# Attention over a cached K and V: scores with the keys on the partitions, exp without the row maximum, row sums from a column of ones in V

## Chip, cores and metric

The kernel runs on one core of a Trainium2 chip. The metric is device microseconds of a whole execution, lower is better. Medians are over all runs of a job, and all ratios below are the mean time of one kernel's fast runs over the mean of the other's fast runs of the same rounds.

Engines: PE is TensorE (PEld its weight loads), DVE VectorE, ACT ScalarE, POOL GpSimd, SP the sync engine that issues DMAs.

## The reference, cut

```python
# two independent problems A and B; B=16, Sq=80, D=576, Hq=32, Hkv=16, Sk=512, Dh=128, bf16
q = (x @ wq).reshape(B, Sq, Hq, Dh)                        # 2 query heads share one K/V head
scores = einsum("bhqd,bhkd->bhqk", q, k) * Dh ** -0.5
p = softmax(scores, axis=-1)
o = einsum("bhqk,bhkd->bhqd", p, v)
out = o.reshape(B, Sq, Hq * Dh) @ wo                       # A and B concatenated on the last axis
```

## The kernel before

The work is cut into 128 "units": one batch and four K/V heads (eight query heads) each. A unit has 4 x 160 rows of queries. The rows are tiled as four tiles of 128 rows, plus one tile that collects the four remainders of 32 rows by column tiling of PE. All operations are listed with a time key; sorting by it gives each engine's program, and semaphore waits are derived from reads and writes.

```python
def em_qk(e, ...):                      # scores: queries on partitions, 512 keys along the free axis
    if k == 0:                          # the four 32-row remainders, in one 128-row tile
        for g4 in range(4):
            last = e.matmul(ps[32*g4:32*g4+32, sbk, :], lhsT=qT[:, qsl, bl, g4*160+128:g4*160+160],
                            rhs=kT[:, ks, :, g4*128:(g4+1)*128], tile_position=(0, 32*g4), ...)
    else:
        last = e.matmul(ps[:, sbk, :], lhsT=qT[...128 rows...], rhs=kT[...], start=True, stop=True)
def em_max(e, ...):  return e.tensor_reduce(negmax[...], ps[:, sbk, :], op=max, negate=True)     # DVE
def em_exp(e, ...):  return e.activation(p_sb[:, psl, :], ps[:, sbk, :], AF.Exp,
                                         bias=negmax[...], accum_out=rowsum[...])                 # ACT
def em_rcp(e, ...):  return e.reciprocal(rinv[...], rowsum[...])                                  # DVE
def em_nrm(e, ...):  return e.tensor_scalar(p_sb[...], p_sb[...], rinv[...], 1.0, mult, mult)     # POOL
def em_tr(e, ...):   # four PE transposes of 128x128: p has to have the keys on partitions
def em_ptev(e, ...): return e.tensor_copy(pT[...], psb[...])                                      # DVE
def em_pv(e, ...):   # four accumulating matmuls, lhsT=V chunk, rhs=pT (160 columns)
# ... [cut] q projection (QB split 480+160 columns), output projection in two passes of 16 heads
S.add("sp", t_k - ..., em_ldk, ...)     # K by DMA transpose, five slots (buffers; NK = 5)
S.add("sp", t_v - ..., em_ldv, ...)     # V, four slots (NV = 4), the same queue
```

## Time and profile before

| | before |
|---|---|
| median of 3 runs | 816.34 us (814.7 to 817.53) |
| span of the profiled run | 812.5 us, granted clock 1.000 |
| PE / DVE / ACT / POOL busy | 98 / 84 / 79 / 53% |
| moved by DMA | 168.5 MB by the kernel's queue |

First, lines of the page of the kernel before: busy times, then rows of 40 equal slices (busy tenths; GB/s), the chain of waits that ended last, and groups (line, engine, operation, tiles, shapes, count, then busy us and mean ns of one, then idle time before it).

```profile
PE 797.9 (98%) x8940; PEld 620.6 (76%) x8940; DVE 680.2 (84%) x1617; ACT 643.4 (79%) x1725; POOL 433.0 (53%) x647
...
PE   7999999999999999999999999999999999999998
...
GB/s 228 243 245 283 249 235 268 260 254 219 190 214 182 224 231 214 207 162 223 180 199 240 245 219 230 237 259 223 224 200 191 200 195 214 199 187 172 156 29 37
...
PE 90%; DVE 5%; DMA 3%; SPq 0%; issue 0%; POOL 0%; ACT 0%; POOLq 0%
...
L452 POOL TENSOR_SCALAR p_sb<-p_sb,rinv 128x512 bf16<-128x512 bf16 x640 | 430.5, 695 | 354.6 <-DVE rinv L449 354.6
L445 ACT ACTIVATE p_sb<-ps,negmax 128x512 bf16<-128x512 f32 x640 | 442.3, 691 | 83.4 <-DVE negmax L441 65.3
L441 DVE TENSOR_REDUCE negmax<-ps 128x1 f32<-128x512 f32 x640 | 434.4, 679 | 4.5 <-PE ps L436 2.9
...
L458 PE MATMUL ps<-ident,p_sb 128*128 128x128 bf16 x2560 | 248.5, 220 | 4.6 <-DVE negmax L441 3.5
```

Everything else stands in PE's shadow: PE's row is all nines but for its two ends, and the chain is 90% PE. The 220 ns of one 128-column transpose is a latency, not a cost, because matmuls overlap: their starts in the trace are 56 ns apart. So PE has to be counted by start-to-start times. Next, the windows view of the same kernel: stretch and its length, busy us of each engine with the number of instructions, granted clock, DMA share, GB/s.

```profile
core 0: us, PE busy (x) PEld busy (x) DVE busy (x) ACT busy (x) POOL busy (x), PEclk, DMA share, GB/s
...
30.00:110.00 80.00, 78.52 (x862) 56.09 (x859) 78.61 (x191) 73.62 (x206) 53.60 (x80) 1.00 1.08 253
110.00:200.00 90.00, 88.75 (x1012) 69.80 (x1009) 74.58 (x176) 74.07 (x200) 47.29 (x71) 1.00 1.08 251
200.00:400.00 200.00, 200.00 (x2262) 156.59 (x2260) 172.05 (x411) 163.88 (x437) 109.50 (x163) 1.00 0.91 204
400.00:530.00 130.00, 130.00 (x1476) 102.06 (x1475) 113.91 (x274) 105.77 (x282) 72.15 (x108) 1.00 1.01 227
```

(The DMA share adds up the times of all packets, so it can pass 1.)

### The profile page before, as it was taken

To read this page: it belongs to the slowest core of one execution; us is meant where nothing else is said; L and a number is where in the kernel's file an instruction comes from. 1 tells how busy PE (TensorE), PEld (TensorE's weight loads), DVE (VectorE), ACT (ScalarE), POOL (GpSimd) and SP (SyncE) were. 2 spreads that over 40 slices of the span, in tenths; PEclk is the share of its full clock that TensorE was granted. 3 is DMA by queue.
4 is the path that set the end of the run, shared out by engine and by line. 5 is a ranking of instruction groups with operands and counts; after the bars stand their busy time and mean duration, and the time that the engine had idled before them with its cause. 6 is when DMAs were issued, how large, how long until landed. Compare 5 with 4: busy or idle time off the path is not lost.

```text
span 812.5 us, 23206 instructions
## 1 busy us (share of the span) xinstructions
PE 797.9 (98%) x8940; PEld 620.6 (76%) x8940; DVE 680.2 (84%) x1617; ACT 643.4 (79%) x1725; POOL 433.0 (53%) x647
## 2 busy tenths in 40 slices
PE   7999999999999999999999999999999999999998
PEld 4677678777777777877777777777777778777778
DVE  3899988888888889888888889888888888988872
ACT  2899888888878778888887887888887788888860
POOL 1466665455555546555555555555465455555650
DMA  9999999999897999979789999999978879977601
GB/s 228 243 245 283 249 235 268 260 254 219 190 214 182 224 231 214 207 162 223 180 199 240 245 219 230 237 259 223 224 200 191 200 195 214 199 187 172 156 29 37
DMA packets 363629, 169.94 MB, mean 209 GB/s; under 512 B 278017, under 2 KB 354305, under 8 KB 363521
## 3 DMA queue, kind: packets, MB, share of 16 engines
q1 hardware_dynamic: 363520, 168.46, 90.9%
q8 instruction: 73, 1.20, 0.6%
q14 instruction: 36, 0.29, 0.1%
HBM read 98.37 MB, written 2.95 MB: 125 GB/s over the span
## 4 chain that ended last, share of the span: by engine, by line
PE 90%; DVE 5%; DMA 3%; SPq 0%; issue 0%; POOL 0%; ACT 0%; POOLq 0%
PE ps L335 20%; PE ps L546 19%; PE ps L458 18%; PE ps L501 16%; PE ps L436 12%; PE ps L431 5%; DVE negmax L441 3%; DVE pT L466 1%; DMA kT<-in_A_k_cache_dram 1%; DMA v_sb<-in_A_v_cache_dram 1%; DMA wq_sb<-in_A_wq_dram 1%; PE ps L259 1%; POOL p_sb L452 0%; SPq L292 0%; DVE rinv L449 0%
## 5 line engine op out<-in xcount | busy, mean ns | idle before, releaser
L452 POOL TENSOR_SCALAR p_sb<-p_sb,rinv 128x512 bf16<-128x512 bf16 x640 | 430.5, 695 | 354.6 <-DVE rinv L449 354.6
L445 ACT ACTIVATE p_sb<-ps,negmax 128x512 bf16<-128x512 f32 x640 | 442.3, 691 | 83.4 <-DVE negmax L441 65.3
L441 DVE TENSOR_REDUCE negmax<-ps 128x1 f32<-128x512 f32 x640 | 434.4, 679 | 4.5 <-PE ps L436 2.9
L466 DVE COPY pT<-ps 128x512 bf16<-128x512 bf16 x512 | 209.3, 409 | 93.3 <-PE ps L458 92.6
L458 PE MATMUL ps<-ident,p_sb 128*128 128x128 bf16 x2560 | 248.5, 220 | 4.6 <-DVE negmax L441 3.5
L501 PE MATMUL ps<-pT,v_sb 128*128 128x160 bf16 x2048 | 225.3, 233 | 2.6 <-DMA v_sb<-in_A_v_cache_dram 1.3
L458 PEld LDWEIGHTS ps<-ident,p_sb 128*128 128x128 bf16 x2560 | 175.4, 98 | 57.2 <-DVE qT L347 21.6
L501 PEld LDWEIGHTS ps<-pT,v_sb 128*128 128x128 bf16 x2048 | 169.0, 98 | 63.9 <-DVE qT L347 3.6
L335 PE MATMUL ps<-xT,wq_sb 128*128 128x480 bf16 (+1 forms) x1280 | 214.4, 300 | 1.6 <-DMA wq_sb<-in_A_wq_dram 0.9
L436 PE MATMUL ps<-kT,qT 128*128 128x512 bf16 x512 | 194.0, 379 | 0.0
L546 PE MATMUL ps<-wo_sb,oT 128*128 128x192 bf16 x1920 | 175.7, 246 | 0.0
L546 PEld LDWEIGHTS ps<-wo_sb,oT 128*128 128x128 bf16 x1920 | 158.6, 98 | 0.0
L335 PEld LDWEIGHTS ps<-xT,wq_sb 128*128 128x128 bf16 x1280 | 107.0, 98 | 45.0 <-DVE qT L347 0.9
L513 ACT CAST oT<-ps 128x320 bf16<-128x320 f32 x256 | 108.9, 425 | 35.2 <-PE ps L501 32.9
L445 ACT ACTIVATION_READ_ACCUMULATOR p_sb<-ps,negmax 128x1 f32 x640 | 128.1, 200 | 0.0
L342 ACT ACTIVATE qT<-ps 128x480 bf16<-128x480 f32 (+1 forms) x128 | 71.8, 561 | 25.6 <-PE ps L335 25.5
L464 DVE COPY pT<-ps 128x512 bf16<-128x512 bf16 x128 | 52.9, 413 | 1.3 <-PE ps L458 1.3
L431 PE MATMUL ps<-kT,qT 128*32 128x512 bf16 x512 | 51.2, 390 | 1.4 <-DMA kT<-in_A_k_cache_dram 1.4
L436 PEld LDWEIGHTS ps<-kT,qT 128*128 128x128 bf16 x512 | 50.1, 98 | 0.7
L347 DVE TENSOR_SCALAR qT<-ps 128x160 bf16<-128x160 f32 (+1 forms) x128 | 41.5, 324 | 3.8 <-PE ps L335 3.7
L566 DVE TENSOR_TENSOR osb<-ps,acc 128x192 bf16<-128x192 f32 x60 | 21.0, 349 | 15.3 <-PE ps L546 12.2
L431 PEld LDWEIGHTS ps<-kT,qT 128*32 128x32 bf16 x512 | 13.1, 92 | 14.9 <-DMA kT<-in_A_k_cache_dram 1.6
(16 smaller groups left out, 77.5 us busy)
## 6 DMA issues: line engine op xcount, KB each, us to landing
v_sb<-in_A_v_cache_dram SPq DMA_DIRECT2D x64, 512.0 KB, 4.5
v_sb<-in_B_v_cache_dram SPq DMA_DIRECT2D x64, 512.0 KB, 4.5
wq_sb<-in_A_wq_dram SPq DMA_DIRECT2D x16, 512.0 KB, 5.5
wq_sb<-in_B_wq_dram SPq DMA_DIRECT2D x16, 512.0 KB, 5.5
wo_sb<-in_A_wo_dram SPq DMA_DIRECT2D x8, 576.0 KB, 5.4
wo_sb<-in_B_wo_dram SPq DMA_DIRECT2D x8, 576.0 KB, 4.8
out_dram<-osb SPq DMA_DIRECT2D x60, 48.0 KB, 2.1
xs<-in_A_x_dram SPq DMA_DIRECT2D x2, 720.0 KB, 5.1
```

The source lines that it names most:

```text
L335: last = e.matmul(ps[:, bank, 0:n1 - n0], lhsT=wq_sb[:, wsl, ck, i * 128:(i + 1) * 128], rhs=xT[:, xsl, ck, n0:n1], start=(ck == 0), stop= ...
L342: return e.activation(qT[:, qsl, b0:b0 + nb, col:col + 80], ps[:, bank, 0:n1 - n0].rearrange("p (b s) -> p b s", b=nb), AF.Identity, scale ...
L431: last = e.matmul(ps[32 * g4:32 * g4 + 32, sbk, :], lhsT=qT[:, qsl, bl, g4 * 160 + 128:g4 * 160 + 160], rhs=kT[:, ks, :, g4 * 128:(g4 + 1) ...
L436: last = e.matmul(ps[:, sbk, :], lhsT=qT[:, qsl, bl, gl * 160:gl * 160 + 128], rhs=kT[:, ks, :, gl * 128:(gl + 1) * 128], start=True, stop ...
L441: return e.tensor_reduce(negmax[:, si:si + 1], ps[:, sbk, :], axis=AX.X, op=AluOpType.max, negate=True)
L445: return e.activation(p_sb[:, psl, :], ps[:, sbk, :], AF.Exp, bias=negmax[:, si:si + 1], scale=1.0, accum_out=rowsum[:, ss, col:col + 1])
L452: return e.tensor_scalar(p_sb[:, psl, :], p_sb[:, psl, :], rinv[:, ss, col:col + 1], 1.0, op0=AluOpType.mult, op1=AluOpType.mult)
L458: last = e.transpose(psb[:, tb, j * 128:(j + 1) * 128], p_sb[:, psl, j * 128:(j + 1) * 128], ident[:])
L466: return e.tensor_copy(pT[:, pts, gl, :, 0:128], psb[:, tb, 0:512].rearrange("p (j n) -> p j n", j=4))
L501: last = e.matmul(ps[:, ob, off:off + 160], lhsT=v_sb[:, vs, gl, j * 128:(j + 1) * 128], rhs=pT[:, pts, gl, j, :], start=(j == 0), stop=(j ...
L513: return e.copy(oT[:, hb:hb + 4, bl * SQ:(bl + 1) * SQ], ps[:, ob, 0:320].rearrange("p (h s) -> p h s", h=4))
L546: last = e.matmul(ps[:, bank, 0:DC], lhsT=oT[:, h, r * 128:(r + 1) * 128], rhs=wo_sb[:, h, c3 * DC:(c3 + 1) * DC], start=(hi == 0), stop=( ...
```

## The change

The intent is to drop the transposes of p. If the scores come out with the keys on the partitions, exp of them is already the operand that P x V needs. Then the row maximum (now along partitions) is not to be had cheaply; it is left out, and a check at the end sends the program to the old code, kept as a general path, if any row sum is out of range. The row sum comes from V widened by a column of ones, and the output is normalised and transposed (5 tiles per unit, instead of 20 tiles of p). Because V needs its 129th column, POOL copies each V into a padded tile. K has four slots instead of five, V three; V is loaded from ACT's queue, and the q projection is split 320+320 columns.

```diff
-NK = 5
-NV = 4
+NK = 4
+NV = 3
+OP_ = 130
...
+        def em_s(e, ts=ts, sbk=sbk):                     # three key chunks of 128, 160 query columns each
+            for c, t in enumerate(ts):
+                last = e.matmul(ps[:, sbk, c * 160:(c + 1) * 160], lhsT=kT[:, U % NK, j, g * 128:(g + 1) * 128],
+                                rhs=qT[:, goct % 2, bl, g * 160:(g + 1) * 160], start=True, stop=True)
+        def em_exp(...): return e.activation(P[:, psl, 0:k, :], ps[...480 columns...], AF.Exp, scale=SCALE)
...
+        add("act", t_v, em_ldv, ...)                     # V from the ACT queue
+        add("pool", t_p, em_vp, ...)                     # v_sb[:, vps, :, 0:128] <- v_in; column 128 is one
+            def em_pv(...):  # x4 per g: lhsT=P[128 rows], rhs=v_sb[..., 0:129]
+        def em_pr(...):      # remainders: 16 matmuls, lhsT=P[..., 128:160], tile_position=(0, 32 * g)
+            def em_rcp(...): return e.reciprocal(rinv[...], ps[:, bank, 128::OP_])
+            def em_nrm(...): return e.tensor_tensor(o_sb[...], src, sc, AluOpType.mult)
+        def em_tr(...):      # five transposes of o_sb
...
+        with e.If_eq(regs[name], 0):                     # the flag says that a row sum was out of range
+            g_run(e, name)                               # the old code
```

## The prediction

> **What bounds the kernel now.** TensorE. The page puts PE at 98% of an 812.5 us span; the windows view shows PE busy 100.0 of 100 us from 200 to 700 us, at granted clock 1.00, while VectorE is at 84%, ScalarE 79%, GpSimd 53%. The chain of waits gives 90% to PE lines, 5% to DVE and 3% to DMA. Busy matmul records overlap, so I cost PE by start-to-start times in the trace: 512 columns 216 ns, 480 203, 192 82, 160 69, 128 56. The Trainium skill, "TensorE: Matmul & The Clock Gate", Back-to-back issue gap, gives N/2.4 + 2.5 ns; the trace agrees to 1 ns. Summed: q projection 174 us, scores of full tiles 111, the 32-row remainder tiles 54, transposes of p 143, PV 142, output projection 158, x transposes 6: 788 us. Remaining 24 us: start (first real matmul at 5.6 us, steady work near 16 us) and small gaps.
>
> The remainder tiles cost more than their columns. Going from a full matmul into the four 32-column ones takes 149 ns instead of 56, and the last of them 322 instead of 216: about 200 ns per visit. The skill's "TensorEngine Tiling (Array Packing)", Key Properties, says changing the tiling mode drains the engine; this trace agrees.
>
> **What the change does.** Removed: 2560 p transposes (143 us of PE), their 640 evictions (262 us DVE), 640 row maxima (434 us DVE), 640 accumulator reads (128 us ACT), 640 GpSimd normalisations (431 us), 256 oT casts on ACT (109 us).
> PE afterwards, by the same rule:
> - scores 2048 x 160 columns: 2048 x 69 = 142 (was 165 with remainders)
> - PV 2048 x 129 columns at 56: 115
> - PV remainders, 16 tiled matmuls of 129 columns per unit: 200 ns of mode change plus four groups estimated at 85 each, 540 ns x 128 = 69 (least certain)
> - transposes of o, 640 x 56: 36
> - q projection 174, output projection 158, x transposes 6, unchanged
> Sum about 700 us, against 788.
>
> Off the path: exp becomes 683 activations of 480 columns without bias pointer or accumulator; an activation of that size takes 569 ns, so about 390 us, plus 128 V-load issues (about 0.43 us each now) on ACT: below 500 us. VectorE: evictions of q, normalisation and oT, about 3 us per unit of 5.5. GpSimd repacks V, 2048 elements; from 695 ns per 512 at most 2.8 us per unit. The V-load issue on ACT waits for that copy, but 12 tiles of lookahead cover about 4 us. DMA moves the same 168 MB, now at about 230 GB/s; before, 40 us stretches reach 273, so it is near but not limiting.
>
> **Time.** 700 us plus the 24 us of start and gaps, plus some 4 us of slower start (V loads compete with the first wq) and 3 us for flag load and branch over the general path: **731 us**, 714 to 762 eight times in ten. Faster by over 2%: 0.96; within 2%: 0.03; slower: 0.01. General path not taken.
>
> **What would show it.** PE still near 98%, DVE near 55%, ACT near 65%; matmul spacing 69 (scores), 56 (PV), no p transposes; remainder block near 0.54 us; every mid-kernel window near 100% PE. Chain almost all PE.
>
> **What would make it wrong.** Tiled weight loads that do not overlap in the PV remainders (up to 0.9 us per unit, +45 us); GpSimd's copy over 4 us, stalling ACT and then PE; K transposes arriving late with four slots rather than five at a 13% higher rate, shown as PE waiting on kT DMA; a failed check, running everything twice.

## The result

| | before | changed | ratio of fast runs |
|---|---|---|---|
| median | 816.22 us (4 runs, the three above among them) | 752.43 us (749.74 to 767.18, 4 runs) | 0.9213, 95% [0.9177, 0.9248] |

It is faster by 8%, inside the predicted range, but 21 us above the predicted 731. The execution profiled first was in the slow state (span 765.4 us, clock 0.972), so the unchanged file was run again for a profile in the fast state. That is the first experiment, and its profile is the one shown here.

Expected of the repetition: 

> The changed kernel once more, for a profile in the fast state. Both theories need it: if the K transposes (or the DMA behind them) are what PE waits for, about 750 us with PE waits on kT of 15 to 30 us and a slower start (scores near 22 us instead of 15); if the 15 us between the slow and the fast runs are only clock, the stalls stay as long as in the slow profile (about 40 us after the start) and only the half-clock time shrinks.

Measured: median 753.98 us (744.57 to 755.01), ratio 0.9251, 95% [0.9221, 0.9282]. Its profiled run, fast, has a span of 742.8 us and is the quickest of its five by 8.5 us; keep that in mind wherever this profile is compared. Lines of its page:

```profile
PE 708.2 (95%) x10093; PEld 619.1 (83%) x10093; DVE 365.2 (49%) x974; ACT 390.9 (53%) x752; POOL 245.3 (33%) x136
...
PE   5987989979999999999999999999999999999996
...
PEclk8998999999999999999999999999999999999999
...
GB/s 253 262 263 266 283 266 249 248 226 243 229 212 234 236 241 245 255 228 191 252 219 253 230 284 267 240 262 273 261 212 241 242 197 269 217 202 186 171 13 35
...
PE 83%; DMA 15%; DVE 1%; SPq 0%; issue 0%; ACT 0%
...
L858 ACT ACTIVATE P<-ps 128x480 bf16<-128x480 f32 (+1 forms) x683 | 374.1, 570 | 304.1 <-PE ps L853 288.7
L887 POOL COPY v_sb<-v_in 128x2048 bf16<-128x2048 bf16 x128 | 242.7, 1896 | 460.5 <-PE ps L919 429.3
L853 PE MATMUL ps<-qT,kT 128*128 128x160 bf16 x2048 | 253.7, 233 | 19.2 <-DMA kT<-in_A_k_cache_dram 16.5
L908 PE MATMUL ps<-v_sb,P 128*128 128x129 bf16 x2048 | 205.4, 222 | 0.0
L919 PE MATMUL ps<-v_sb,P 128*32 128x129 bf16 x2048 | 54.3, 226 | 0.0
```

DMA's share of the chain went from 3 to 15%, and PE's row has dents, all but the last in its first quarter. The windows of the same run, beside those of before, say where:

```profile
core 0: us, PE busy (x) PEld busy (x) DVE busy (x) ACT busy (x) POOL busy (x), PEclk, DMA share, GB/s
...
30.00:110.00 80.00, 68.71 (x978) 57.27 (x976) 41.21 (x108) 45.11 (x85) 29.95 (x16) 0.94 1.16 267
110.00:200.00 90.00, 84.81 (x1211) 74.54 (x1209) 42.25 (x111) 47.49 (x95) 28.44 (x15) 0.98 1.17 242
200.00:400.00 200.00, 200.00 (x2921) 176.44 (x2918) 105.39 (x282) 112.44 (x214) 70.16 (x37) 1.00 1.03 230
400.00:530.00 130.00, 126.93 (x1846) 111.49 (x1835) 66.60 (x180) 70.10 (x134) 43.87 (x24) 1.00 1.18 260
```

Between 30 and 110 us PE stands still for 11 us while DMA moves 267 GB/s, the most of these four stretches. The longest such wait, in the timeline (start, length, engine, line, what; in brackets the idle time before it and what ended it):

```profile
45.68 9.87 SPq L880 DMA_TRANSPOSE kT<-in_A_k_cache_dram  x1
...
53.38 0.41 PE L908 MATMUL ps<-v_sb,P 128*128 128x129 bf16 x4
...
60.27 0.56 PE L853 MATMUL ps<-qT,kT 128*128 128x160 bf16 x3 [6.48 <-DMA kT<-in_A_k_cache_dram]
...
60.62 1.54 PE L798 MATMUL ps<-xT,wq_sb 128*128 128x320 bf16 x5
```

The issue of one K transpose holds the sync queue for 9.87 us (its median in this run is 3.9), PE finds no K, and after 6.48 us of waiting the next five q projection matmuls of 320 columns take 1.54 us where they take 0.84 elsewhere in this run. That is the clock. The clock records of the trace have 6.8 us at 0.5 from 58.2 us on, and further ones after the waits at 98 and 158 us: 24.5 us at half clock in all, of which about 11 belong to the cold start and the end. The Trainium skill, "TensorE: Matmul & The Clock Gate", Part 1, says that an idle window drops PE to half clock; this trace agrees. So a wait on DMA is paid twice, once while PE stands and once while it is cold. In the slow profile the waits and other gaps over 0.45 us add up to 47.7 us against 31.5 in the fast one, and the half clock to 44.8 against 24.5 us. Of the two readings in the expectation the first held: in the fast profile PE waits 19.2 us for K and the first scores come at 21.3 us, and the stalls shrank together with the half clock.

### The profile page after: what moved, and what is told of

It reads as the page before. It is cut to its first block, busy times and chain, and to the rows that moved or that the text cites. A ratio compares the mean times of both kernels' runs of the same rounds, so it can differ in the third digit from the quotient of the medians.

```text
span 765.4 us, 22766 instructions
## 1 busy us (share of the span) xinstructions
PE 714.9 (93%) x10093; PEld 623.6 (81%) x10093; DVE 365.2 (48%) x974; ACT 390.7 (51%) x752; POOL 244.9 (32%) x136
## 3 DMA queue, kind: packets, MB, share of 16 engines
q10 hardware_dynamic: 67584, 67.12, 31.5%
HBM read 98.37 MB, written 2.95 MB: 132 GB/s over the span
## 4 chain that ended last, share of the span: by engine, by line
PE 81%; DMA 17%; SPq 0%; DVE 0%; ACT 0%; issue 0%
PE ps L798 20%; PE ps L980 19%; PE ps L853 17%; PE ps L908 15%; DMA kT<-in_A_k_cache_dram 11%; PE ps L919 5%; DMA kT<-in_B_k_cache_dram 4%; PE ps L945 3%; DMA xs<-in_A_x_dram 1%; DMA out_dram<-osb 1%; PE ps L946 1%; PE ps L736 1%; ACT P L858 0%; SPq L767 0%; DVE qT L805 0%
## 5 line engine op out<-in xcount | busy, mean ns | idle before, releaser
L858 ACT ACTIVATE P<-ps 128x480 bf16<-128x480 f32 (+1 forms) x683 | 373.8, 570 | 325.5 <-PE ps L853 310.2
L887 POOL COPY v_sb<-v_in 128x2048 bf16<-128x2048 bf16 x128 | 242.3, 1893 | 483.3 <-PE ps L919 443.4
L853 PE MATMUL ps<-qT,kT 128*128 128x160 bf16 x2048 | 255.5, 235 | 31.6 <-DMA kT<-in_A_k_cache_dram 24.9
L798 PE MATMUL ps<-xT,wq_sb 128*128 128x320 bf16 x1280 | 220.9, 305 | 3.4 <-DVE qT L805 2.9
L908 PE MATMUL ps<-v_sb,P 128*128 128x129 bf16 x2048 | 206.8, 223 | 0.0
L853 PEld LDWEIGHTS ps<-qT,kT 128*128 128x128 bf16 x2048 | 161.3, 98 | 50.9 <-issue 33.7
L805 DVE CAST qT<-ps 128x320 bf16<-128x320 f32 x248 | 121.4, 489 | 91.3 <-PE ps L798 91.2
L908 PEld LDWEIGHTS ps<-v_sb,P 128*128 128x128 bf16 x2048 | 144.3, 99 | 15.8
L935 DVE TENSOR_TENSOR o_sb<-ps,rinv 128x384 bf16<-128x384 f32 (+1 forms) x256 | 125.6, 491 | 8.8
L945 PE MATMUL ps<-ident,o_sb 128*128 128x128 bf16 x512 | 50.7, 222 | 0.8 <-DVE o_sb L935 0.7
L945 PEld LDWEIGHTS ps<-ident,o_sb 128*128 128x128 bf16 x512 | 36.6, 100 | 1.2 <-DVE o_sb L935 1.1
L946 PE MATMUL ps<-ident,o_sb 128*128 128x128 bf16 x128 | 28.5, 223 | 0.0
```

The lines of the kernel that those rows point to most:

```text
L798: last = e.matmul(ps[:, bank, 0:320], lhsT=wq_sb[:, wsl, ck, i * 128:(i + 1) * 128], rhs=xT[:, xsl, ck, n0:n1], start=(ck == 0), stop=(ck ...
L805: return e.copy(dst, src) if ev == "act" else e.tensor_copy(dst, src)
L853: last = e.matmul(ps[:, sbk, c * 160:(c + 1) * 160], lhsT=kT[:, U % NK, j, g * 128:(g + 1) * 128], rhs=qT[:, goct % 2, bl, g * 160:(g + 1) ...
L858: return e.activation(P[:, psl, 0:k, :], ps[:, sbk, 0:k * 160].rearrange("p (c n) -> p c n", c=k), AF.Exp, scale=SCALE)
L887: return e.tensor_copy(v_sb[:, vps, :, 0:128], v_in[:, vs, :, :].rearrange("p g (j d) -> p (g j) d", j=4))
L908: last = e.matmul(ps[:, bank, off:off + 129], lhsT=pap(16 * U + 4 * g + j, 0, 128), rhs=v_sb[:, vps, 4 * g + j, 0:129], start=(j == 0), st ...
```

## The experiments

Three theories. A: in the first 16 units, which have no output projection and so cost PE only about 4.1 us each, PE asks for more bytes per us than DMA delivers. B: PE's own work, or ACT held up by V issue and V copy, is dearer than I counted. C: something in how K is brought in is at fault: its fourth slot, V on a second queue, or the bursts of weights in front of it. "Unit 16 at" below is the start of the first score matmul of unit 16, and "gaps" the sum of start-to-start times of matmuls over 0.45 us.

| run | median us | ratio to before (95%) | unit 16 at | gaps us |
|---|---|---|---|---|
| changed, again | 753.98 | 0.9251 [0.9221, 0.9282] | 101.8 | 31.5 |
| no V (wrong) | 719.18 | 0.8821 [0.8793, 0.8849] | 88.1 | 9.7 |
| V on the sync queue | 747.60 | 0.9171 [0.9133, 0.9210] | 105.1 | 36.6 |
| start reordered | 761.54 | 0.9341 [0.9301, 0.9381] | 110.3 | 44.5 |
| five K slots | 753.07 | 0.9211 [0.9171, 0.9252] | 99.4 | 36.1 |
| weights spread | 753.10 | 0.9172 [0.9107, 0.9238] | 106.5 | 33.7 |
| no V in front (wrong) | 738.50 | 0.9051 [0.9011, 0.9091] | 88.2 | 27.2 |
| four output passes | 774.47 | 0.9443 [0.9371, 0.9515] | 104.9 | 46.8 |
| V on sync, late spread | 762.55 | 0.9319 [0.9264, 0.9374] | 104.5 | 47.5 |
| four passes, mended | 747.81 | 0.9170 [0.9150, 0.9190] | 103.7 | 26.6 |
| both of these | 745.66 | 0.9150 [0.9127, 0.9174] | 105.7 | 30.1 |
| four passes, late spread, V on ACT | 737.69 | 0.9003 [0.8973, 0.9032] | 108.2 | 24.5 |

"Unit 16 at" and "gaps" are each read from one profiled execution. The unchanged file has two: 101.8 us and 31.5 us of gaps in the quick one of the table, 107.6 and 47.7 in the slow one profiled first. So a difference of that size between two rows shows little by itself; the times and ratios carry more.

The runs came in four jobs on different chips; the first four rows, the next four, the next three and the last each shared a job and its runs of before.

### Without V

```diff
-        add("act", t_v, em_ldv, ...)
+        if U < NV:
+            add("act", t_v, em_ldv, ...)      # later units use what lies in the slot
```

> Wrong result on purpose: V is loaded for the first three units only, so 64 of 168 MB are gone from the DMA engines; PE, ACT, DVE and GpSimd do the same work. Theory A (DMA delivery, not engine work, is the missing 20 us): 712 to 722 us, waits on kT under 3 us, clock 1.00 after the start. Rival B (PE work itself costs more than my 700 us, or ACT stalled by V issue and copy): stays at 740 us or more.

719.18 us, and no wait on K is left. The windows of this run:

```profile
core 0: us, PE busy (x) PEld busy (x) DVE busy (x) ACT busy (x) POOL busy (x), PEclk, DMA share, GB/s
...
30.00:110.00 80.00, 80.00 (x1206) 68.41 (x1204) 49.48 (x130) 54.33 (x104) 35.78 (x19) 1.00 1.01 195
110.00:200.00 90.00, 90.00 (x1317) 79.52 (x1315) 46.09 (x122) 50.92 (x101) 31.10 (x17) 1.00 0.72 151
200.00:400.00 200.00, 200.00 (x2910) 176.70 (x2909) 105.08 (x282) 111.26 (x213) 69.24 (x37) 1.00 0.72 145
400.00:530.00 130.00, 130.00 (x1897) 114.83 (x1894) 68.29 (x182) 73.78 (x144) 45.49 (x25) 1.00 0.76 156
```

PE is full everywhere, with 1206 matmuls between 30 and 110 us where the changed kernel manages 978. The start-to-start times, waits over 0.45 us left out, add up to 700.0 us: the sum that I predicted. So PE's work is not the missing time. This run also says what PE would ask for at full speed. From 30 to 100 us it takes 8.83 MB of K and 4.87 MB of the rest; with as much V as K that is (2 x 8.83 + 4.87) / 70 us = 322 GB/s, an estimate. The changed kernel got 268 GB/s in this stretch. From 200 to 400 us the same reckoning gives 242 GB/s, and there it does not wait.

The run takes ACT's V issues and their wait for the POOL copy away as well, so that part of B is not refuted yet. The next run does that.

### V on the sync queue

```diff
-        add("act", t_v, em_ldv, ...)
+        add("sp", t_v, em_ldv, ...)
```

> V loads issued from the sync queue behind K, as before the change, in place of the ACT queue. Theory C (V from a second queue slows the K transposes that PE needs first): 10 to 20 us faster, K issue time back under 4 us. Theory A (total demand in a stretch exceeds what the DMA engines deliver): the same within 1%, since bytes are the same. If the sync queue itself is the limit (K issues alone take 566 us of it), slower: 760 us or more.

747.60 us: 0.9% better than the changed kernel (0.9171 against 0.9251), less than C asked for, about what A allowed. The issue of K takes 4.15 us on average against 4.23, so K does not get through faster. ACT now neither issues V nor waits for the copy, and PE still waits 23.8 us for K: ACT was not what held PE up. Unit 16 comes at 105.1 us, no earlier. The V issues did not make the sync queue a worse limit; that it is no limit is not shown (see "Still open" below).

### The start reordered

```diff
-        t_v = ... if U >= NV else -789.0 + 3 * U
+        t_v = ... if U >= NV else -69.4 + 2.0 * U       # first V loads after the first q evictions
-            t = ... else (-100.0 + blk if blk < 3 else -80.0 + blk)
+            t = ... else (-100.0 + blk if blk < 3 else -64.5 + blk)
```

> Only the start is reordered: the first three V loads are issued after the first q evictions rather than at once, and the last two x blocks are transposed after the first half of the q projection. The x load that PE now waits 7.2 us for should then cost nothing: first scores near 15 us instead of 22.4, and 5 to 8 us off the whole time if nothing later eats it; under 2 us if the first 16 units are bound by DMA anyway (theory A), because then the bytes, not the start of PE, set when unit 16 is reached.

A miss, and an instructive one. The first scores came at 18.3 us instead of 21.3, and yet the run is slower: 761.54 us, with unit 16 at 110.3 instead of 101.8 us. With 1.5 MB of V held back at the start DMA carried 256 GB/s instead of 281 between 5 and 30 us, and 247 instead of 268 between 30 and 100. PE started sooner and waited longer. A had asked for no gain, not for a loss; and that DMA carried fewer bytes per us while PE waited more speaks against a fixed ceiling in bytes. Why this run is slower stays open.

### Five K slots

```diff
-NK = 4
-NG = 14
+NK = 5
+NG = 11
-    warm = sb("warm", [128, 512], BF16)
+    warm = oT[:, 0, 0:512]
```

> Five K slots as before the change, in place of four (room from P groups 14 to 11 and the warm-up tile laid over oT). Rival (my prediction's own warning: one K slot fewer makes K late): most of the 30 us between the changed kernel and the run without V come back, 725 to 735 us. Theory A (in the first 16 units DMA delivers its 265 GB/s and cannot do more): unit 16 still begins near 100 us, only the later short waits shrink, 744 to 752 us.

753.07 us, the same (just above the 744 to 752 that A had asked for). The slot that the change took away, which my prediction named as the danger, is not the cause. The trace of the changed kernel agrees: for each of units 8 to 19 the issue of K began 2.7 to 10.6 us after the last matmul that read its slot, so the slot was free and the sync queue was not. Lines of the sync queue in that run (start, length), one issue right after another:

```profile
76.53 12.00 SPq L880 DMA_TRANSPOSE kT<-in_A_k_cache_dram  x3
88.58 1.94 SPq L767 DMA_DIRECT2D wq_sb<-in_A_wq_dram  x2
90.56 5.46 SPq L880 DMA_TRANSPOSE kT<-in_A_k_cache_dram  x1
96.07 0.58 SPq L773 DMA_DIRECT2D wq_sb<-in_A_wq_dram  x1
96.70 15.31 SPq L880 DMA_TRANSPOSE kT<-in_A_k_cache_dram  x4
```

### Weights spread

```diff
-    ... for d_ in (0.0, 4.0, 8.0))          # time keys of the wq loads; a unit has 16
+    ... for d_ in (0.0, 32.0, 64.0))
-    add("sp", x + 3.0 * WSP * wc, em_ldwo, ...)
+    add("sp", x + 48.0 * wc, em_ldwo, ...)
```

> Same bytes; wq and wo chunks spread over more units (wq 32 instead of 4 tiles apart, wo 48 instead of 24). If bursts of wq and wo in the sync queue hold up K: the waits after unit 16 (about 10 us in the fast profile, near 150, 430 and 510 us) vanish, 738 to 746 us. If only the sum of bytes matters, the first 16 units stay as long (16 units in 80 us) and the total is within 1%.

753.10 us, no different in total, but the parts moved. After 190 us there is no gap left but the one at the very end: from unit 40 to the last score matmul the run takes 470.5 us, exactly as without V, against 474.3 in the changed kernel. Two lines of its windows view:

```profile
400.00:500.00 100.00, 100.00 (x1456) 88.23 (x1454) 52.56 (x143) 55.32 (x103) 34.95 (x19) 1.00 1.15 261
500.00:600.00 100.00, 100.00 (x1456) 88.49 (x1454) 52.78 (x140) 56.28 (x110) 35.16 (x19) 1.00 1.15 251
```

Unit 32 begins at 208.4 us here, at 195.7 in the quick profile of the changed kernel and at 206.5 in its slow one, so whether spreading cost time in front is not shown. There are two sorts of waits: late ones, near 430 and 510 us, come from the order and bunching of loads, as spreading removed them with the same bytes; early ones are not cured by it.

### No V in the front

```diff
+        vu = vs if U < 18 else U                      # units 3 to 17 load no V
+        if vu == U:
             add("act", t_v, em_ldv, ...)
```

> Wrong result on purpose: V is not loaded for units 3 to 17, all later units load it. Theory A puts most of the loss into the first 16 units: unit 16 begins near 88 us as without any V (fast profile of the changed kernel 101.8), total 730 to 738 us. If the loss were spread evenly over the kernel, only 3 to 5 us come back.

738.50 us, half a us above the expected range. Unit 16 begins at 88.2 us, as without any V. Of the 35 us between the changed kernel and the run without V, 15 to 16 come from the loads of these 15 units alone (738.5 against 754.0). The rest lies later: this run still waits from 130 to 150 us and from 420 to 500 us. So it is V's loads that cost the time in front, as A says; but the front is not all.

### Four output passes

If PE has too little to do in front, give it some: the output projection in four passes of 8 heads, two short pieces per unit, from unit 9 on instead of 17.

```diff
-        for hh in range(2):
+        for hh in range(4):
...
-                    t, bank = 16.0 * (u_a + 1 + n) + 13.2, PB
+                    t, bank = 16.0 * (u_a + 1 + n // 2) + (5.2 if n % 2 == 0 else 13.2), PB
...
+                    return e.tensor_tensor(a_, ps[:, bank, 0:DC], a_, AluOpType.add)   # passes 1 and 2
```

> Output projection in four passes of 8 heads instead of two of 16, two short ones per unit, so that PE work starts at unit 9 instead of 17 and the last tail is 10 us instead of 20. DVE gets 120 more adds of 0.35 us. Theory A (PE has too little work per unit, 4.1 us, while DMA needs 5 us per unit in the first 16 units): the time lost in front shrinks, 738 to 746 us. If DMA is not what bounds the front, the same 750 or slower by the extra evictions.

774.47 us, worse. But the front did what A said: with 96 matmuls of the output projection (7.9 us at 82 ns) done before it, unit 16 comes at 104.9 us, only 3 us later, and the gaps between 22 us and unit 16 fell from 13.0 to 7.1 us. (In the three later runs with four passes these gaps are 6.2, 12.5 and 11.7 us, so this is weak evidence.) The loss is elsewhere. VectorE waits 38.2 us for output DMAs, up to 8.7 us at a time, with only two output slots and the stores in the sync queue among the K transposes; and PE waits 19.6 us for those evictions, since the output projection has one PSUM bank, one of the eight buffers that matmuls write into (4.8 us at 236 us, 7.4 at 418, 4.9 at 606). From its view of waits (total us, times, longest):

```profile
DVE osb L1004 <- DMA out_dram<-osb: 38.2, 14, 8.7
...
PE ps L980 <- DVE osb L1004: 19.6, 8, 7.2
```

### V on the sync queue, and the spread only in the second half

```diff
-        add("act", t_v, em_ldv, ...)
+        add("sp", t_v, em_ldv, ...)
...
+    ((0.0, 32.0, 64.0) if goct > 5 else (0.0, 4.0, 8.0))
+    x + (48.0 if prob else 24.0) * wc
```

> V on the sync queue, and the spread wq and wo loads only from the second half of the kernel on (smoothing took all waits out of units 48 to 127, 471 us there as without V, but lengthened units 8 to 32). If both effects hold and add: 3 to 7 us below V on sync alone (747.6), 740 to 745 us, units 48 to 127 in 471 to 474 us. If the waits are one budget of DMA time that only moves about: 746 to 752.

Where the expectation says "units 48 to 127", its 471 us are those from unit 40 on; I had miscounted. A clear miss: 762.55 us, and 492 us from unit 40 to the end instead of 471. Two edits, each harmless alone, hurt together: with K, V and the weights all in one queue in program order, the waits near 420 to 570 us grew instead of vanishing.

### The four passes, mended

Four output slots, stores from ACT's queue, and own semaphores for the quarters of wo.

```diff
-    osb = sb("osb", [128, 2, DC], BF16)
+    osb = sb("osb", [128, 4, DC], BF16)
-                    add("sp", t + 3.0, em_st, ...)
+                    add("act", t + 3.0, em_st, ...)
```

> The quarter passes again, with what I take to have spoiled them removed: four output slots instead of two, stores from the ACT queue instead of behind the K transposes of the sync queue, own semaphores for the wo quarters. If the store wait (38 us of DVE waits on output DMA) was the reason for 774 us, now 735 to 747 us and PE waits on the output projection gone; theory A then also wants unit 32 reached with 10 us more PE work done. If the quarter passes themselves cost (PSUM bank, extra evictions), 755 or more.

747.81 us, just outside the expected range. The wait for output DMAs fell from 38.2 to 1.8 us and the waits of the output projection for evictions are gone, so the store waits were the reason for the 774 us; which of the three edits cured them was not tried.

```profile
DVE osb L1004 <- DMA out_dram<-osb: 1.8, 3, 0.7
```

The gaps after unit 16 are 3.1 us at 153 and 1.4 us at 162 us, and the late ones again (6 us at 423, 2 us at 513).

### Both together

> Both together. The bound without any V wait is 719 us less about 3 us of shorter tail stalls; I expect 730 to 742 us if the parts add, and no better than the better of the two if one DMA budget is behind all.

The edit is the sum of the last two. 745.66 us: outside the range, hardly better than the mended passes alone (the two intervals overlap), as the second reading, one DMA budget, had said. It waits 21.5 us for K, again in many small pieces after 450 us.

### Four passes, late spread, V on ACT

The two runs with V in the sync queue and spread weights had late waits; the spread run with V on ACT had none. So the last run is the mended four passes, with the late spread, and V left where the change had put it.

> V stays on the ACT queue; four output passes with four slots; wq and wo spread only in the second half. The spread run with V on ACT had no K wait after unit 48, the same with V on the sync queue had many. If that difference is the sync queue's order (V and spread loads stand in front of K there), this run has under 3 us of PE waits after 400 us and takes 730 to 740 us, the best of all. If the clean second half of that run was only its later arrival there (its own delay of 12 us before unit 32 had filled the buffers), waits near 420 and 510 us stay and it takes 744 to 750 us.

737.69 us, ratio 0.9003 to before: the best of all, and inside the range that the first reading expected. It differs from "both together" (0.9150) in V's queue alone and moves the same bytes, so the waits are not one budget of DMA time. Its waits on DMA and two windows follow. First, for comparison, the waits on K of the changed kernel:

```profile
PE ps L853 <- DMA kT<-in_A_k_cache_dram: 16.5, 6, 6.5
...
PE ps L853 <- DMA kT<-in_B_k_cache_dram: 2.7, 3, 1.1
```

```profile
PE ps L853 <- DMA kT<-in_A_k_cache_dram: 14.7, 6, 7.2
...
PE ps L736 <- DMA xs<-in_A_x_dram: 6.9, 2, 6.5
```

```profile
core 0: us, PE busy (x) PEld busy (x) DVE busy (x) ACT busy (x) POOL busy (x), PEclk, DMA share, GB/s
...
30.00:110.00 80.00, 69.60 (x1003) 59.59 (x1002) 36.95 (x98) 45.38 (x90) 28.40 (x15) 0.96 1.20 241
...
400.00:530.00 130.00, 130.00 (x1893) 114.83 (x1891) 75.95 (x203) 76.28 (x143) 45.44 (x24) 1.00 1.17 264
```

From 400 to 530 us PE is full while DMA carries 264 GB/s, more than the changed kernel's 260 with waits. No wait on K of problem B is left at all. What stays is the front: 10 us of idle PE between 30 and 110 us, as in the changed kernel. The rival that the expectation names, a later arrival with full buffers, has the slow profile of the changed kernel against it: that reached unit 32 at 206.5 us, later than this run's 201.5, and still had 10 us of gaps between 432 and 529 us.

Still open: whether the front is a ceiling in bytes or in the rate at which K's transposes get through. In the runs that waited there (30 to 100 us) DMA carried anything from 235 to 271 GB/s, so there is no single ceiling to be named, and every run that cured the front also removed V traffic. The sync queue, which brings K in one issue after another, was issuing for 69.0 of these 70 us in the changed kernel, 68.5 with V in it, 62.8 without V and 68.4 already before the change. One K issue takes 3.9 us (median) with V's loads beside it and 2.3 without them. So the front can as well be told as a queue of K issues that V's traffic makes longer. A kernel that brings K in without the DMA transpose would tell; it wasn't tried. Nor do these runs explain why two executions of the same kernel wait 10 us more or less.

## Why the prediction was right, and where its sum was off

- **PE bound, work 788 us falling to 700.** Right. The run without V shows 700.0 us (704.1 in the changed kernel's quick profile, by the same count). That the sum meets the predicted one so exactly is luck, for the count includes the warm-up and work at half clock, and the parts were off a little both ways: P x V matmuls have a median start distance of 59 ns where I took 56, and the remainder block cost 450 ns per unit where I took 540. The trace shows its 16 starts in groups of four, 62 to 66 ns from group to group (I took 85), with 93 ns extra on entry and about 100 on leaving. The Trainium skill's "TensorEngine Tiling (Array Packing)", Key Properties, says a mode change drains PE; both kernels' traces agree.
- **Other engines out of the way.** Right. exp took 570 ns (predicted 569), POOL's copy 1.9 us (at most 2.8), DVE was busy 49% and ACT 53% (55 and 65). ACT waiting for POOL's copy was not a cause, as the run with V on the sync queue shows.
- **Flag and branch, 3 us.** Right. From the sync engine's branch at 739.6 us to its last drain at 742.5 us are 2.9 us, where the kernel before needed 0.2. The Trainium skill's "Runtime: NRT & Kernel Launch", Instruction fetch mechanics, says that a taken branch to a page not loaded stalls for a fetch; these traces agree with that: between the two the instruction queues carry 32 KB, at the end of the kernel before nothing.
- **"24 us of start and gaps" plus 4 us of slower start: too much.** Without V the whole remainder beside the 700 us is 17 us of a 716.9 us span. Part of the 24 had been small waits near the end of the old kernel, nine gaps of 0.66 to 1.14 us between 741 and 786 us, which are gone. The slower start itself was under-counted (first scores at 21.3 instead of 15.0 us).
- **The step that failed:** "DMA moves the same 168 MB, now at about 230 GB/s; before, 40 us stretches reach 273, so it is near but not limiting." 230 is the mean over the kernel. The first 16 units have no output projection, so PE runs through them faster than through any others, and at the pace without V they ask for 322 GB/s. The changed kernel got 268 there. I compared a mean demand with a peak supply; the peak demand was to be compared with it. The prediction's own test, "every mid-kernel window near 100% PE", failed at 68.7 of 80 us. The term was zero in the prediction and measured 35 us (754.0 - 719.2): about 15 come from the V loads of units 3 to 17, the rest from later ones; of those, spreading the same bytes, with V on ACT's queue, cured what lay after 400 us. That V's traffic makes PE wait for K is shown; whether bytes or K issues ran short in front is not.
- **The warning that came near it** named the right symptom, PE waiting for K, and the wrong cause, the lost K slot. Five slots changed nothing.

The 731 us thus came out of two errors of opposite sign: 12 us too many for start and gaps (731 against 719 with V's traffic gone), and 35 us too few for DMA. That they offset each other in part is luck.

## What to carry to other kernels

When an edit shortens the engine that bounds a kernel, recompute the bandwidth that the transfers then need stage by stage, above all for the stage in which that engine has least to do; the mean over the kernel hides it. To see whether waits on a transfer are bytes or order, run the kernel once with a stream of loads taken away and once with the same bytes spread: here the first cured all waits on K and the second only the late ones, and those only with V on its own queue. Look at how long the issuing queue is busy, too. And look at the clock beside a wait: in these runs every PE pause of over 3.1 us was followed by 2.6 to 5.8 us at half speed.

## What the Trainium skill lacked or had wrong

- "TensorE: Matmul & The Clock Gate", Part 3, says in its list of what overlaps that weight loads overlap running matmuls only where the row group differs. The 16 tiled matmuls of the remainders all use all rows, and groups of four still follow each other at 62 to 66 ns, 8 to 12 ns more than 129 columns at the page's 2.4 GHz, so hardly any of their weight loads shows. (Elsewhere in Parts 2 and 3 the page also allows it for a background buffer; the list leaves that out.)
- The same page advises no PE pauses over about 3 us. A start-to-start gap of 2.12 us (at 513 us, the mended four passes) and one of 2.47 us (at 516 us, both edits together) were each followed by 3.4 us at half clock. Over all profiles of the changed kernel and its variants, after the first 25 us, half clock followed all 35 gaps of over 3.1 us and 8 of the 23 between 2.0 and 3.1 us; one of 2.95 us (at 557 us, V on sync and late spread) had none after it.
- "TensorEngine Tiling (Array Packing)" says that a mode change drains, but not what that costs: here 93 ns on entry and about 100 ns on leaving.
- The pages give rates for DMA transposes and for plain copies, each alone; none gives what DMA delivers for a mixture of the two. Here it was 235 to 271 GB/s between 30 and 100 us in the runs in which PE waited for it, and issuing one K transpose held the sync queue 3.9 us (median) with the V loads running and 2.3 us without them.
